# Attention decode on one core: the two heads of a tile on separate partition halves, one load each, and scores read at a smaller stride

## The chip, the cores and the metric

The kernel runs on one core of one Trainium2 chip. The metric is the device time of one execution in microseconds (us). Every experiment was timed beside the kernel before on the same chip.

Names used throughout: PE is TensorE (matmuls), PEld its weight loads, DVE is VectorE, ACT is ScalarE, POOL is GpSimd, SP is SyncE, which issues the loads. "Partition" means one of the 128 rows of the on-chip memory SBUF. "L330" is a line of the kernel file; matmuls are recorded by two helpers, so all ordinary matmuls share one line and are told apart by their tiles. The changed kernel is one line longer above the helpers, so L330, L334 and L660 of before are L331, L335 and L661 of after, and L332 and L662 in some experiments.

## The reference, cut to what matters

One decoding step for four sequences. Only the last 4096 of 16384 cached keys count. An FFN runs beside the attention, and a sigmoid gate mixes the two.

```python
def _A_ref(x, k_cache, v_cache, wq, wo):          # B=4, 32 query heads, 8 key heads, Dh=128
    W = min(4096, max(256, Sk // 4))              # 4096
    q = (x @ wq).reshape(B, 1, 32, 128)...        # transposed to B, heads, 1, 128
    k = repeat(k_cache[:, :, Sk - W:, :], 4, axis=1)
    v = repeat(v_cache[:, :, Sk - W:, :], 4, axis=1)
    scores = einsum("bhqd,bhkd->bhqk", q, k) * (Dh ** -0.5)
    o = einsum("bhqk,bhkd->bhqd", softmax(scores), v)
    return o.reshape(B, 1, 4096) @ wo
# b = ReGLU FFN of B_x (512 -> 1792 -> 512)
# result: g * a + (1 - g) * b, g = sigmoid(sum(x * gate_w))
```

Keys and values together are 67.1 MB, all weights 13.9 MB. Each byte is used for very little arithmetic, so the loads are the first thing to look at; the profile below shows that they set the pace.

## The kernel before

The work is cut into 16 tiles. A tile is one batch and two neighbouring key heads, with 2 MB of keys and 2 MB of values; two tiles make a set, and there are 8 sets. For each tile:

- one load of keys puts 64 keys of one head (16 KB) on each partition, with the two heads interleaved: partition 2r+h holds rows r of head h;
- PE transposes the tile as fp32 pairs of bf16, 32 products of 128x128, and DVE or ACT copies them back over the loaded keys;
- the score products of a set read those transposed keys, four column groups of PE at a time; DVE evicts them to `sc` with a running maximum; ACT computes the exponentials into `pe`, which is interleaved with zeros for the other head;
- PE transposes the probabilities and multiplies them with the value tile.

The parts that the change touches (cuts marked):

```python
def _pe_order():
    ...
        o += [("SC", s), ("OQ", i - 3), ("PV", i - 2), ("SW", s)]       # per set s; PV is the value tile
    ...

# in sync(): the loads
                load(("K", i), f"d_k{i % KSLOTS}", Ksb[:, i % KSLOTS, :],
                     A_k_cache[b, h:h + 2, SK - WIN:SK, :].rearrange("h (r c) d -> r h (c d)", r=64), waits=w)
    ...
                src = A_v_cache[b, h:h + 2, SK - WIN:SK, :].rearrange("h (r c) d -> r h (c d)", r=64)
                    load(("V", i), f"d_v{slot}", Vsb[:, slot, :], src, waits=w)
    ...

# in tensor(): the score products of set s
            for f in range(4):
                ...
                for e in range(2):
                    for j in range(4):
                        jp, pair = j // 2, j % 2              # jp: which head of the tile
                        ...
                        rhs = kt2((2 * s + pair) % KSLOTS)[:, 8 * f:8 * f + 8, jp:128:2, e]
                        mm(bk[32 * j:32 * j + 8, :], qblk[:, g, 8 * e:8 * e + 8], rhs, e == 0, e == 1,
                           ..., pos=(0, 32 * j))

# in scalar(): the exponentials, one for each head's 64 rows
        pev = pe[:, :].rearrange("p (k u) -> p k u", u=2)
                a.activation(pev[r, :, n], sc[r, :], ACTF.Exp, ...)
```

In `rhs`, `e` picks one bf16 of an fp32 pair and `jp:128:2` every second partition of the tile, so neighbouring elements lie 8 bytes apart.

## Time and profile before

| what | before | where it is read |
|---|---|---|
| time | 213.43 us at first, 213.54 us beside the changed kernel | timed runs |
| DMA engines busy | full from slice 2 to slice 36 of 40 | the page's slices |
| rate of the loads | about 425 GB/s | slices, window view |
| a 16 KB packet (one partition's row of a tile) | 0.61 us | DMA records of the trace |
| PE busy | 75% | the page's first part |
| PE waits for key loads | 17.3 us | view of waits |
| a score product | 629 ns (median) | view of one tile |

The first lines are the page of the kernel before: the span, the busy time of each engine, then a digit (busy tenths) or a rate for each of 40 equal slices of the span, and last the share of each engine in the chain of work that ended last.

```profile
span 209.9 us, 5524 instructions
...
PE 157.9 (75%) x2526; PEld 112.2 (53%) x2526; DVE 121.5 (58%) x279; ACT 69.8 (33%) x62; POOL 4.3 (2%) x19
...
DMA  5999999999999999999999999999999999998200
GB/s 206 419 456 400 419 433 419 434 437 417 428 395 408 440 422 425 434 425 428 418 434 418 428 428 425 436 409 426 425 431 422 428 431 425 425 418 353 81 0 4
...
PE 48%; DMA 25%; ACT 13%; DVE 9%; issue 2%; SPq 2%; ACTq 0%; DVEq 0%
```

The DMA engines never run dry before slice 37, and they move about 425 GB/s. The 35 full slices of 5.25 us at that rate are 78 of the 81 MB that have to be moved. The last line seems to say otherwise: PE holds 48% of the chain. The chain goes back through the wait of a load for its buffer, and so through PE, although many other loads were still under way.

The groups of instructions on the page of before: line, engine, operation, output<-input, shapes, count, then busy us, mean ns of one, and the engine's idle time just before them with what ended most of it.

```profile
L334 PE MATMUL bank<-identf,Ksb 128*128 128x128 f32 x512 | 72.5, 306 | 22.6 <-DMA Ksb<-in_A_k_cache_dram 17.3
...
L660 ACT ACTIVATE pe<-sc,negmax 64x2048 bf16<-64x2048 bf16 x16 | 41.6, 2600 | 49.1 <-DVE negmax L586 48.9
L330 PE MATMUL bank<-Ksb,qblk 128*8 128x512 bf16 x256 | 30.9, 623 | 4.7 <-DVE Ksb L533 4.7
```

These are the key transposes, the exponentials and the score products. The score products are 30.9 / 8 = 3.9 us of PE for each set.

The view of the key tile, for the score products of before (after the count: shortest, median and longest duration in ns):

```profile
L330 PE MATMUL bank<-Ksb,qblk x256: 608/629/662, 35.9 to 187.4; 128*8 128x512 bf16 x128
```

The waits of the queue's own engine in before (us in total, times, longest):

```profile
SPq L254 <- PE bank L330: 126.6, 10, 32.4
```

SP waits 126.6 us for PE to free buffers. That costs nothing, because enough loads are already queued, as the loads themselves show (issues on the page of before: count, KB each, median us from issue to landing):

```profile
Ksb<-in_A_k_cache_dram SPq DMA_DIRECT2D x16, 2048.0 KB, 25.0
Vsb<-in_A_v_cache_dram SPq DMA_DIRECT2D x15, 2048.0 KB, 31.7
Wbig<-in_A_wq_dram SPq DMA_DIRECT2D x1, 4096.0 KB, 16.5
```

2 MB at 425 GB/s are 4.9 us, and a key tile lands 25 us after its issue, so about five tiles are always in the queue.

### The profile page before, as it was taken

The numbers are of one execution on the slowest core, as the hardware profiler recorded it, in microseconds if no ns is written. First come the engines' busy times: TensorE is split into PE (matmuls) and PEld (weight loads), VectorE is DVE, ScalarE is ACT, GpSimd is POOL, SyncE is SP. The second block draws the span as 40 slices with busy tenths as digits, with TensorE's granted clock in tenths as the row PEclk, the third lists the DMA queues.
The fourth block names the chain that finished last, engine by engine and source line by source line (L and its number), as shares of the span: only waits on it lengthen the run. The fifth ranks groups of instructions, "written<-read, shape, count | busy, mean of one in ns | idle before, by whom it ended". The sixth has DMA issues, their size and how long they took to land.

```text
span 209.9 us, 5524 instructions
## 1 busy us (share of the span) xinstructions
PE 157.9 (75%) x2526; PEld 112.2 (53%) x2526; DVE 121.5 (58%) x279; ACT 69.8 (33%) x62; POOL 4.3 (2%) x19
## 2 busy tenths in 40 slices
PE   0373708889997129897896989698969899994784
PEld 0361506268376029276745947594759347842731
DVE  3180784789659005695678468736873647962312
ACT  2000411195036004172509143613362345508100
POOL 7000000000000000000000000000000000000000
PEclk9997976999999955997999799859975999998569
DMA  5999999999999999999999999999999999998200
GB/s 206 419 456 400 419 433 419 434 437 417 428 395 408 440 422 425 434 425 428 418 434 418 428 428 425 436 409 426 425 431 422 428 431 425 425 418 353 81 0 4
DMA packets 6839, 81.37 MB, mean 388 GB/s; under 512 B 792, under 2 KB 800, under 8 KB 2336
## 3 DMA queue, kind: packets, MB, share of 16 engines
q1 hardware_dynamic: 6816, 81.01, 91.5%
q8 instruction: 20, 0.33, 0.6%
q14 instruction: 3, 0.02, 0.0%
HBM read 81.01 MB, written 0.00 MB: 386 GB/s over the span
## 4 chain that ended last, share of the span: by engine, by line
PE 48%; DMA 25%; ACT 13%; DVE 9%; issue 2%; SPq 2%; ACTq 0%; DVEq 0%
PE bank L330 32%; DMA Ksb<-in_A_k_cache_dram 17%; PE bank L334 17%; ACT pe L660 13%; DMA Wbig<-in_A_wq_dram 8%; DVE Ksb L533 4%; DVE pe L565 2%; SPq L254 2%; DVE qblk L557 1%; DVE osb L600 1%; DVE negmax L586 0%; DVE osum L623 0%; DVE hmax L584 0%; DVE oq L607 0%; ACTq L95 0%
## 5 line engine op out<-in xcount | busy, mean ns | idle before, releaser
L334 PE MATMUL bank<-identf,Ksb 128*128 128x128 f32 x512 | 72.5, 306 | 22.6 <-DMA Ksb<-in_A_k_cache_dram 17.3
L533 DVE COPY Ksb<-bank 128x1024 bf16<-128x1024 bf16 x104 | 66.3, 685 | 33.6 <-PE bank L334 32.8
L334 PEld LDWEIGHTS bank<-identf,Ksb 128*128 128x128 f32 x512 | 66.4, 160 | 26.8 <-issue 10.2
L660 ACT ACTIVATE pe<-sc,negmax 64x2048 bf16<-64x2048 bf16 x16 | 41.6, 2600 | 49.1 <-DVE negmax L586 48.9
L637 ACT ACTIVATE Ksb<-bank 128x1024 bf16<-128x1024 bf16 x24 | 24.3, 1023 | 55.1 <-PE bank L334 55.1
L330 PE MATMUL bank<-Ksb,qblk 128*8 128x512 bf16 x256 | 30.9, 623 | 4.7 <-DVE Ksb L533 4.7
L575 DVE TENSOR_SCALAR_CACHE_REDUCE sc<-bank 128x512 bf16<-128x512 f32 x32 | 22.1, 692 | 14.0 <-PE bank L330 14.0
L330 PE MATMUL bank<-Vsb,pT 128*8 128x128 bf16 x1024 | 21.9, 245 | 2.3 <-issue 2.3
L330 PEld LDWEIGHTS bank<-Vsb,pT 128*8 128x8 bf16 x1024 | 17.9, 96 | 3.1 <-issue 2.7
L330 PEld LDWEIGHTS bank<-Ksb,qblk 128*8 128x8 bf16 x256 | 4.5, 88 | 25.0 <-DVE sc L575 13.4
L330 PE MATMUL bank<-sel,pe 128*128 128x32 bf16 x256 | 8.0, 181 | 11.6 <-ACT pe L660 11.3
L600 DVE TENSOR_SCALAR osb<-bank,recip 128x128 bf16<-128x128 f32 x16 | 5.6, 351 | 16.0 <-PE bank L330 15.5
L591 DVE CAST pT<-bank 128x512 bf16<-128x512 f32 x16 | 10.3, 685 | 6.6 <-PE bank L330 6.6
L330 PEld LDWEIGHTS bank<-sel,pe 128*128 128x128 bf16 x256 | 7.2, 99 | 12.8 <-DVE oq L607 8.2
L330 PE MATMUL bank<-Wbig,oq 128*4 128x512 bf16 x32 | 8.6, 425 | 0.7 <-DVE oq L607 0.7
L330 PEld LDWEIGHTS bank<-oneh,osb 128*32 128x32 bf16 x256 | 4.6, 115 | 7.0 <-issue 4.0
L330 PE MATMUL bank<-oneh,osb 128*32 128x2 bf16 x256 | 5.3, 176 | 1.3 <-DVE osb L600 1.3
L330 PE MATMUL bank<-rowsum,wsum 128*128 128x1 f32 x32 | 6.0, 292 | 0.0
L330 PE MATMUL bank<-Wbig,xT 128*4 128x512 bf16 x32 | 3.4, 603 | 3.4 <-DMA Wbig<-in_A_wq_dram 3.4
L330 PEld LDWEIGHTS bank<-rowsum,wsum 128*128 128x128 f32 x32 | 5.5, 242 | 0.1
L330 PEld LDWEIGHTS bank<-Wbig,oq 128*4 128x4 bf16 x32 | 2.7, 92 | 5.3 <-issue 1.8
L648 ACT ACTIVATE ge<-bank 4x1 f32<-4x1 f32 x2 | 0.2, 152 | 13.5 <-PE bank L330 13.5
(51 smaller groups left out, 47.5 us busy)
## 6 DMA issues: line engine op xcount, KB each, us to landing
Ksb<-in_A_k_cache_dram SPq DMA_DIRECT2D x16, 2048.0 KB, 25.0
Vsb<-in_A_v_cache_dram SPq DMA_DIRECT2D x15, 2048.0 KB, 31.7
Wbig<-in_A_wq_dram SPq DMA_DIRECT2D x1, 4096.0 KB, 16.5
Wbig<-in_A_wo_dram SPq DMA_DIRECT2D x1, 4096.0 KB, 31.5
Vsb<-in_A_v_cache_dram SPq DMA_DIRECT2D x4, 512.0 KB, 24.9
Vsb<-in_B_W_gate_dram SPq DMA_DIRECT2D x1, 1792.0 KB, 24.3
Vsb<-in_B_W_up_dram SPq DMA_DIRECT2D x1, 1792.0 KB, 33.1
Vsb<-in_B_W_down_dram SPq DMA_DIRECT2D x1, 1792.0 KB, 41.0
```

Source lines behind the costliest of these rows:

```text
L254: E.op(lambda: e.dma_start(dst, src), ev=ev, waits=waits, ctr=ctr)
L330: E.op(lambda: t.matmul(out_, lhsT, rhs, start=start, stop=stop, tile_position=pos, skip_group_check=True), ev=ev, waits=waits)
L334: E.op(lambda: t.transpose(out_, in_, idn), ev=ev, waits=waits)
L533: E.op(lambda: v.tensor_copy(kt_dst(i, f), bankb[tr(key)]), ev=("E",) + key, waits=[key])
L557: E.op(lambda r=r, u=u, b=b: v.tensor_copy(qv[r, b, n, :, :, :, u], src[r, :, :, b, :]), ev=("E",) + key if lastop else None, waits=[key, ...
L565: E.op(lambda n=n: v.memset(pev[64 * n:64 * n + 64, :, 1 - n], 0.0), ev=("PEZ",) if n else None, waits=[("QT", 1)])
L575: E.op(lambda: v.tensor_scalar(sc[:, 512 * f:512 * f + 512], banks[scb(key)], 1.0, None, op0=ALU.mult, op1=ALU.max, accum_out=mx4[:, f:f + ...
L591: E.op(lambda: v.tensor_copy(pT[:, s % 2, 512 * f:512 * f + 512], banks[tr(key)]), ev=("E",) + key, waits=[key] + ([("PV", 2 * s - 3)] if ...
L600: E.op(lambda: v.tensor_scalar(osb[:, i % 2, :], banks[OB][:, 0:128], recip[:, i % 4:i % 4 + 1], None, op0=ALU.mult), ev=("NORM", i), wait ...
L637: E.op(lambda: a.activation(kt_dst(i, f), bankb[tr(key)], ACTF.Copy), ev=("E",) + key, waits=[key])
L648: E.op(lambda u=u: a.activation(ge[:, u:u + 1], banks[ACC][0:4, 0:1], ACTF.Exp, scale=-1.0 if u == 0 else 1.0), ev=("GE",) if u else None, ...
L660: E.op(lambda r=r, n=n: a.activation(pev[r, :, n], sc[r, :], ACTF.Exp, bias=negmax[r, s % 2:s % 2 + 1], scale=SCALE, accum_out=rowsum[r, s ...
```

## The change

The intent is to make PE's reads of the keys denser. If head 0 lies on partitions 0 to 63 and head 1 on 64 to 127, the columns of one head are neighbours after the transpose, and the score products read at stride 2 (4 bytes) and not at stride 4 (8 bytes). Each tile then takes two loads of 1 MB, one for each head. The scores of a set are issued in two halves, with the output step and a value tile between them, so that PE has work while scores are evicted. The probabilities lie in blocks of 64 in place of every second element. The diff, cut to its core:

```diff
@@ _pe_order
-        o += [("SC", s), ("OQ", i - 3), ("PV", i - 2), ("SW", s)]
+        o += [("SC", s, 0), ("OQ", i - 3), ("PV", i - 2), ("SC", s, 1), ("SW", s)]
@@ sync, keys (values alike, also the pieces of the last tile)
-                load(("K", i), f"d_k{i % KSLOTS}", Ksb[:, i % KSLOTS, :],
-                     A_k_cache[b, h:h + 2, SK - WIN:SK, :].rearrange("h (r c) d -> r h (c d)", r=64), waits=w)
+                for j in range(2):
+                    load(("K", i, j), f"d_k{i % KSLOTS}", Ksb[64 * j:64 * j + 64, i % KSLOTS, :],
+                         A_k_cache[b, h + j, SK - WIN:SK, :].rearrange("(r c) d -> r (c d)", r=64), waits=w)
+                plan.ev[("K", i)] = plan.ev[("K", i, 1)]
@@ tensor, scores
-            for f in range(4):
+            for f in (2 * half, 2 * half + 1):
...
-                        rhs = kt2((2 * s + pair) % KSLOTS)[:, 8 * f:8 * f + 8, jp:128:2, e]
+                        rhs = kt2((2 * s + pair) % KSLOTS)[:, 8 * f:8 * f + 8, 64 * jp:64 * jp + 64, e]
@@ vector (memsets) and scalar (exponentials)
-        pev = pe[:, :].rearrange("p (k u) -> p k u", u=2)
+        pev = pe[:, :].rearrange("p (k u r) -> p k u r", u=2, r=64)
```

More of the change, by code (lines that the diff above doesn't have):

```diff
@@ L141, in _pe_order @@
 def _pe_order():
-    o = [("KT", 0), ("XT",), ("Z",), ("Q",), ("QT",), ("KT", 1), ("SC", 0), ("SW", 0)]
-    o += [("KT", 2), ("GU",), ("PT", 0), ("RS", 0), ("KT", 3), ("HT",), ("SC", 1), ("FFN",), ("SW", 1), ("PV", 0)]
+    o = [("KT", 0), ("XT",), ("Z",), ("Q",), ("QT",), ("KT", 1), ("SC", 0, 0), ("SC", 0, 1), ("SW", 0)]
+    o += [("KT", 2), ("GU",), ("PT", 0), ("RS", 0), ("KT", 3), ("HT",), ("SC", 1, 0), ("FFN",), ("SC", 1, 1), ("SW", 1), ("PV", 0)]
     for s in range(2, NSET):
@@ L222, in _program @@
         elif k == "SC":
-            for f in range(4):
+            for f in (2 * it[2], 2 * it[2] + 1):
                 scf[("SC", it[1], f)] = len(scf)
@@ L285, in sync @@
                     w += {WG_SLOT: [("GU", 1)], WU_SLOT: [("GU", 1)], WD_SLOT: [("FFN",)]}.get(slot, [])
-                src = A_v_cache[b, h:h + 2, SK - WIN:SK, :].rearrange("h (r c) d -> r h (c d)", r=64)
-                if i < NPAIR - 1:
-                    load(("V", i), f"d_v{slot}", Vsb[:, slot, :], src, waits=w)
-                else:
-                    n = TILE // VPIECES
-                    for p in range(VPIECES):
-                        load(("V", i, p), f"d_vl{p}", Vsb[:, slot, p * n:(p + 1) * n],
-                             src[:, :, p * n:(p + 1) * n], waits=w if p == 0 else [])
+                n = TILE // (VPIECES if i == NPAIR - 1 else 1)
+                for p in range(TILE // n):
+                    for j in range(2):
+                        src = A_v_cache[b, h + j, SK - WIN:SK, :].rearrange("(r c) d -> r (c d)", r=64)
+                        load(("V", i, p, j), f"d_v{slot}" if i < NPAIR - 1 else f"d_vl{p}",
+                             Vsb[64 * j:64 * j + 64, slot, p * n:(p + 1) * n], src[:, p * n:(p + 1) * n], waits=w)
+                    plan.ev[("V", i, p)] = plan.ev[("V", i, p, 1)]
         E.op(lambda: e.dma_start(out.rearrange("b o d -> (b o) d"), osum[0:4, :]), ev=("OUT",), waits=[("OSUM",)],
@@ L375, in QT, with SC @@
                        waits=tr_free(key) + [("E", "Q", n), ("QD", n)])
-        def SC(s):
+        def SC(s, half):
             b, qq = set_of(s)
-            for f in range(4):
+            for f in (2 * half, 2 * half + 1):
                 key = ("SC", s, f)
@@ L392, in SC @@
                            ev=key if lastmm else None, waits=w if (e, j) == (0, 0) else (), pos=(0, 32 * j))
-            plan.ev[("SCL", s)] = plan.ev[("SC", s, 3)]
+            plan.ev[("SCL", s)] = plan.ev[("SC", s, f)]
         def PT(s):
@@ L410, in PV @@
                     w = [("E", "PT", s, 0), ("INIT",)] + ([("NORM", i - 1)] if i else [])
-                    w += [("V", i)] if i < NPAIR - 1 else []
+                    w += [("V", i, 0)] if i < NPAIR - 1 else []
                 if ch == 32:
@@ L495, in _program @@
         elif k == "SC":
-            dve += [("ESC", it[1], f) for f in range(4)] + [("MAX", it[1])]
+            dve += [("ESC", it[1], f) for f in (2 * it[2], 2 * it[2] + 1)] + [("MAX", it[1])] * it[2]
         elif k == "SW":
@@ L562, in PEZ @@
         def PEZ():
-            pev = pe[:, :].rearrange("p (k u) -> p k u", u=2)
+            pev = pe[:, :].rearrange("p (k u r) -> p k u r", u=2, r=64)
             for n in range(2):
-                E.op(lambda n=n: v.memset(pev[64 * n:64 * n + 64, :, 1 - n], 0.0), ev=("PEZ",) if n else None,
+                E.op(lambda n=n: v.memset(pev[64 * n:64 * n + 64, :, 1 - n, :], 0.0), ev=("PEZ",) if n else None,
                      waits=[("QT", 1)])
@@ L632, in scalar @@
         E = _Eng(plan, a, "act")
-        pev = pe[:, :].rearrange("p (k u) -> p k u", u=2)
+        pev = pe[:, :].rearrange("p (k u r) -> p k u r", u=2, r=64)
         def EKT(i, f):
@@ L659, in EXP @@
                 w = [("NEGMAX", s), ("E", "SC", s, 3)] + ([("PT", s - 1, 1)] if s else []) + ([("RS", s - 2)] if s >= 2 else [("PEZ",)])
-                E.op(lambda r=r, n=n: a.activation(pev[r, :, n], sc[r, :], ACTF.Exp, bias=negmax[r, s % 2:s % 2 + 1],
+                E.op(lambda r=r, n=n: a.activation(pev[r, :, n, :], sc[r, :].rearrange("p (k r) -> p k r", r=64), ACTF.Exp, bias=negmax[r, s % 2:s % 2 + 1],
                                                    scale=SCALE, accum_out=rowsum[r, s % 2:s % 2 + 1]),
```

## The prediction

> **What bounds it now.** The loads. The page's slices show the DMA engines full and about 425 GB/s from the second slice to the 36th of 40; 81 MB at that rate are 190 us of a 209.9 us span. In the trace's DMA records a 16 KB packet (one partition's row of a tile) takes 0.61 us: 26.8 GB/s an engine, 429 for sixteen. The chain of waits names PE for 48%, but the DMA queue's own waits (127 us on PE) only delay issues: a key tile lands 25 us, a value tile 32 us after its issue, five or six tiles are always queued, and the engines never run dry. After the loads comes a tail: the last value pieces land near 195 to 198 us, the rest is PE and DVE work.
>
> **What the change removes.** Keys are read at 4 bytes instead of 8 between neighbours. Today a set's 32 score products take 3.85 us; four start together, each group 0.44 us after the last (timeline, 165 to 169 us), and every bank then waits for an eviction of 0.69 + 0.08 us. If stride 2 makes a group 0.22 us, evictions (4 x 0.77 = 3.1 us) become the limit, and the value tile between the halves fills that wait. Estimate: 1.5 to 2 us of PE a set, some 14 us in all, plus up to 3 us in the two early memsets (1.76 us each). Nearly all of it is off the critical path, since the loads set the pace; at most 3 to 5 us of the tail could be won. Exponentials and evictions keep their sizes.
>
> **What it adds.** Some 36 more DMA issues of about 0.5 us on the sync queue: hidden. But every key and value load now writes 64 partitions, first 0 to 63, then 64 to 127, in order in the same queue. [...]
>
> **Sum (estimate).** 13.9 MB of weights at 427 GB/s: 33 us. [...] With 2 us of start and 8 us of tail, 351 to 301 us. I expect about 312 us, 1.46 times the 213.43 us; range 245 to 355 us. Chances: slower by over 2% 0.84, within 2% 0.07, faster 0.09.
>
> **What would show it.** GB/s in the slices down to 220 to 280 while the DMA share stays high; 16 KB packets near 1.0 to 1.2 us; waits of PE's transposes on the key loads grown from 17 us to 80 or more; PE busy below 60%; the weight loads unchanged. Apart from that, score products (median 629 ns) near 300 to 400 ns and a set's score work below 3.3 us of PE.
>
> **What would make it wrong.** [...] the rate remains above 400 GB/s, and the shorter PE work gives 204 to 213 us.

The marked cuts take out what no trace of before shows: why a load on one half of the partitions would run slower, and at which rates. The sum came to 351 to 301 us, with the point at 312 us. One of its terms is cut, that of the 67.1 MB of keys and values; the terms that are left (33 us of weights, 2 us of start, 8 us of tail) make 43 us. No load of before writes only a half, and the prediction said itself that this step was unproved. It also counted on a relief: engines that have drifted to opposite halves were to run at full rate again. That was the author's guess; the trace of before shows only the drift, since the sixteen completions of one load spread over 0.5 us at first (8.0 to 8.5 us of the span) and over 4.0 us late (158.5 to 162.4 us). The conditions cut from the last paragraph are that half loads are not slower at all, or that the relief comes early and stays.

## More of the kernel before

The window view of before, 80 to 165 us of the span (its first line names the columns):

```profile
core 0: us, PE busy (x) PEld busy (x) DVE busy (x) ACT busy (x) POOL busy (x), PEclk, DMA share, GB/s
80.00:165.00 85.00, 73.08 (x1194) 56.39 (x1193) 57.48 (x128) 35.96 (x31) 0.00 (x0) 0.86 1.01 425
```

In this steady stretch PE is busy for 73 of 85 us and the DMA engines for all of it, at 425 GB/s.

## The result, and the profile after

The changed kernel took 350.2 us (median of 4 runs, 348.84 to 353.36) against 213.54 us (213.19 to 214.29) of the kernel before on the same chip. The ratio is 1.641, with a 95% interval of 1.629 to 1.653. Here and below a ratio is the mean time of one kernel's fast runs over that of the other's fast runs in the same rounds, so it is not quite the ratio of the medians that are quoted. The result is correct.

The page of after, the same parts:

```profile
span 346.1 us, 5566 instructions
...
PE 169.8 (49%) x2526; PEld 133.8 (39%) x2526; DVE 121.2 (35%) x279; ACT 61.2 (18%) x62; POOL 4.3 (1%) x19
...
DMA  8999999999999999999999999999999999999810
GB/s 182 319 347 252 265 312 206 308 218 214 204 347 285 214 216 216 237 233 231 229 220 223 225 223 228 218 235 220 228 254 259 267 254 261 279 271 247 210 47 0
...
DMA 63%; PE 20%; another core or an unknown queue 11%; SPq 2%; DVE 2%; issue 1%; DVEq 0%
```

The DMA row is as full as before, but the rate row is not: from slice 14 to 29 it averages 225 GB/s. The busy share says that the engines always have a packet in hand; it does not say that they move it at full speed. The higher early slices (319, 347, 312) are those with weight loads, which still span all 128 partitions: from 14 to 22 us of the span, with query weights under way, 393 GB/s are moved. The instruction counts of PE are the same, and PE's share of busy time fell from 75% to 49%.

The groups of after:

```profile
L335 PE MATMUL bank<-identf,Ksb 128*128 128x128 f32 x512 | 88.2, 353 | 115.6 <-DMA Ksb<-in_A_k_cache_dram 115.5
...
L661 ACT ACTIVATE pe<-sc,negmax 64x2048 bf16<-64x2048 bf16 x16 | 32.0, 1999 | 67.0 <-DVE negmax L587 66.8
...
L331 PE MATMUL bank<-Ksb,qblk 128*8 128x512 bf16 x256 | 22.3, 463 | 5.1 <-DVE Ksb L534 4.7
```

The transposes now wait 115.5 us for key loads; it was 17.3. The exponentials went from 2600 to 1999 ns and the score products from 623 to 463 ns on average. So what the change was made for came true. The value products wait too (waits of after, us in total, times, longest):

```profile
PE bank L335 <- DMA Ksb<-in_A_k_cache_dram: 115.5, 15, 21.7
...
PE bank L331 <- DMA Vsb<-in_A_v_cache_dram: 37.3, 14, 5.4
```

The view of the key tile of after, for the score products:

```profile
L331 PE MATMUL bank<-Ksb,qblk x256: 385/388/634, 39.4 to 317.7; 128*8 128x512 bf16 x128
```

The median is 388 ns; some are up to 634 ns. The granted clock averages 0.70 in the window from 100 to 300 us of after, where PE often waits, against 0.86 in the steady stretch of before, and the transposes have grown to 353 ns as well. That the clock explains both was not tested.

```profile
100.00:300.00 200.00, 98.54 (x1494) 81.08 (x1481) 70.36 (x157) 37.30 (x36) 0.00 (x0) 0.70 1.01 240
```

The loads on the page of after:

```profile
Ksb<-in_A_k_cache_dram SPq DMA_DIRECT2D x32, 1024.0 KB, 43.2
Vsb<-in_A_v_cache_dram SPq DMA_DIRECT2D x30, 1024.0 KB, 55.7
Wbig<-in_A_wq_dram SPq DMA_DIRECT2D x1, 4096.0 KB, 20.2
```

Half the size, and yet a key load lands 43 us after its issue, where the whole tile took 25. From the DMA records of the traces, the time of one packet in ns (5% / median / 95%), for this and for the experiments below:

```
16 KB packets   before              611 /  613 /  621
                after               822 / 1166 / 1288
                e2_opposite         966 / 1200 / 1274
                e4_values_only      611 / 1132 / 1288
                e8, both queues     909 / 1075 / 1283
                e9_stride_2         611 /  612 /  620
                e10, 114 to 138 us 1787 / 2104 / 2412
```

A packet of the same size takes about twice as long after the change. The extra time agrees with that: 67.1 MB at 426 GB/s are 157.5 us; with the 136.7 us that were added they are 294 us, which would be 228 GB/s (an estimate that puts the whole difference on the keys and values).

### The profile page after: what moved, and what is told of

Same layout as the page of the kernel before. It is cut to its first block, busy times and chain, and to the rows that moved or that the text cites. A ratio compares the mean times of both kernels' runs of the same rounds, so it can differ in the third digit from the quotient of the medians.

```text
span 346.1 us, 5566 instructions
## 1 busy us (share of the span) xinstructions
PE 169.8 (49%) x2526; PEld 133.8 (39%) x2526; DVE 121.2 (35%) x279; ACT 61.2 (18%) x62; POOL 4.3 (1%) x19
## 4 chain that ended last, share of the span: by engine, by line
DMA 63%; PE 20%; another core or an unknown queue 11%; SPq 2%; DVE 2%; issue 1%; DVEq 0%
DMA Ksb<-in_A_k_cache_dram 49%; DMA Vsb<-in_A_v_cache_dram 14%; PE bank L331 10%; PE bank L335 9%; SPq L254 2%; DVE Ksb L534 1%; DVE sc L576 0%; DVE osum L624 0%; DVE osb L601 0%; DVE oq L608 0%; DVE rowmax L580 0%; DVEq L67 0%
## 5 line engine op out<-in xcount | busy, mean ns | idle before, releaser
L335 PE MATMUL bank<-identf,Ksb 128*128 128x128 f32 x512 | 88.2, 353 | 115.6 <-DMA Ksb<-in_A_k_cache_dram 115.5
L335 PEld LDWEIGHTS bank<-identf,Ksb 128*128 128x128 f32 x512 | 84.2, 190 | 118.5 <-issue 62.4
L534 DVE COPY Ksb<-bank 128x1024 bf16<-128x1024 bf16 x104 | 68.7, 688 | 142.7 <-PE bank L335 142.1
L661 ACT ACTIVATE pe<-sc,negmax 64x2048 bf16<-64x2048 bf16 x16 | 32.0, 1999 | 67.0 <-DVE negmax L587 66.8
L331 PE MATMUL bank<-Vsb,pT 128*8 128x128 bf16 x1024 | 24.1, 260 | 37.5 <-DMA Vsb<-in_A_v_cache_dram 37.3
L331 PEld LDWEIGHTS bank<-Vsb,pT 128*8 128x8 bf16 x1024 | 19.7, 102 | 39.5 <-DMA Vsb<-in_A_v_cache_dram 34.0
L331 PE MATMUL bank<-Ksb,qblk 128*8 128x512 bf16 x256 | 22.3, 463 | 5.1 <-DVE Ksb L534 4.7
L331 PE MATMUL bank<-Wbig,oq 128*4 128x512 bf16 x32 | 10.9, 510 | 0.6 <-DVE oq L608 0.6
L331 PEld LDWEIGHTS bank<-Ksb,qblk 128*8 128x8 bf16 x256 | 6.1, 96 | 13.2 <-DVE Ksb L534 6.1
L331 PE MATMUL bank<-rowmax,perm 128*128 128x1 bf16 x8 | 1.4, 180 | 8.7 <-DVE rowmax L580 8.7
## 6 DMA issues: line engine op xcount, KB each, us to landing
Wbig<-in_A_wq_dram SPq DMA_DIRECT2D x1, 4096.0 KB, 20.2
```

The source lines that it names most:

```text
L331: E.op(lambda: t.matmul(out_, lhsT, rhs, start=start, stop=stop, tile_position=pos, skip_group_check=True), ev=ev, waits=waits)
L335: E.op(lambda: t.transpose(out_, in_, idn), ev=ev, waits=waits)
L534: E.op(lambda: v.tensor_copy(kt_dst(i, f), bankb[tr(key)]), ev=("E",) + key, waits=[key])
L661: E.op(lambda r=r, n=n: a.activation(pev[r, :, n, :], sc[r, :].rearrange("p (k r) -> p k r", r=64), ACTF.Exp, bias=negmax[r, s % 2:s % 2 + 1],
```

## The experiments

The theory at this point: the cost lies in where the rows of a load stand. Loads that write only partitions 0 to 63, or only 64 to 127, move at 225 GB/s in the middle slices of after; loads over all 128 move at 425 in before. The rivals: (A) it is the number of loads, their size, or the order in which the cache is read; (B) it is something else in the change, such as the order on PE or the layout of the probabilities. The theory also had a second part, the relief, which was a guess: when the engines drift apart, some write the first half while others write the second, and the two groups should not disturb each other. All the experiments below but e1 gave correct results.

### e1: the changed kernel with loads over the full width

The same 32 loads of 1 MB for the keys, from the same addresses, but each over 128 partitions, with half rows of 8 KB. The keys then stand in the wrong place, and the result is wrong (relative error 0.729).

```diff
-    load(("K", i, j), ..., Ksb[64 * j:64 * j + 64, i % KSLOTS, :],
-         A_k_cache[b, h + j, SK - WIN:SK, :].rearrange("(r c) d -> r (c d)", r=64), waits=w)
+    load(("K", i, j), ..., Ksb[:, i % KSLOTS, 4096 * j:4096 * j + 4096],
+         A_k_cache[b, h + j, SK - WIN:SK, :].rearrange("(r c) d -> r (c d)", r=128), waits=w)
# values alike
```

> The changed kernel with one thing undone: each of its two loads a tile writes all 128 partitions (half of the columns) instead of 64 partitions; same number of loads, 1 MB each, from the same contiguous source of one head. The result is wrong on purpose (keys and values lie in other places). Theory [...]: 205 to 212 us, 420 GB/s or more, 8 KB packets near 0.31 us. Rival A (two smaller loads a tile, or reading one head's contiguous region at a time, is what costs): 330 us or more, as in the changed kernel. Whatever it gives is also the worth of the change without its loads.

It took 210.95 us (209.46 to 212.52), a ratio of 0.9884 (0.9811 to 0.9956) to before. From its page, the rates, the score products and the key loads:

```profile
GB/s 217 488 402 396 439 413 426 421 417 424 416 414 407 420 421 421 418 419 421 419 422 421 416 421 424 416 418 421 416 421 421 421 418 419 418 424 398 253 9 1
...
L332 PE MATMUL bank<-Ksb,qblk 128*8 128x512 bf16 x256 | 18.4, 389 | 5.0 <-DVE Ksb L535 4.7
...
Ksb<-in_A_k_cache_dram SPq DMA_DIRECT2D x32, 1024.0 KB, 22.9
```

The whole loss is gone. Rivals A and B are out: the number of loads, their size and their source are the same, and so is the rest of the change. The rest of the change is worth 1.2%. PE's score work fell from 30.9 to 18.4 us, 12.5 us in all, and the time fell by some 2.5 us, because PE did not set the pace.

### e2 and e3: two groups of engines on opposite halves

If the relief is real, it can be forced. The second head is loaded first, and the first load of the kernel is cut so that 8 engines get more of it than the other 8; from then on one group should stay ahead and write one half while the other writes the other half. In e2 the extra is 4 rows for each of the 8 engines, half of an engine's 8 rows of a tile (128 rows over the sixteen engines whose completions the trace shows); in e3 it is 8 rows, a whole tile.

```diff
-    for j in range(2):
+    for j in (1, 0):
+        # tile 0, j == 1, e2: rows 0:32 in one load, rows 32:64 in four loads of 8 rows, 4 apart
+        #   Ksb[96 + t:125 + t:4, ...] <- src[32 + t:61 + t:4]            for t in 0..3
+        # e3: all 64 rows in eight loads of 8 rows, 4 apart
+        #   Ksb[64 + g:93 + g:4, ...] <- src[g:g + 29:4]                  for g in 0..3, 32..35
```

> The changed kernel, still 64 partitions a load. Second head first, and 32 of the first load's 64 rows go on 8 engines alone, so that these 8 run half a tile behind the other 8 from the start. Theory [...] the rate is near 400 GB/s at first and falls with drift: 215 to 260 us. Rival B (a load of 64 partitions runs at half rate for a reason that has nothing to do with which engines are in the same half[...]): 335 to 355 us.

> As e2, but all 64 rows of the first load go on the 8 engines, so that these run a whole tile (both halves) behind. Theory: a whole period is no offset[...]: 325 to 350 us. If e2 was fast for having a few odd loads at the start, or for engines merely being apart, this is as fast as e2.

This missed altogether. e2 took 358.97 us (357.22 to 360.87), a ratio of 1.680 (1.672 to 1.689): slower than the changed kernel itself. e3 took 357.36 us in its fast run; its profiled run of 363.96 us was slow, so it adds nothing but that it is no better. The completions in e2's trace show two groups of eight engines some 2.8 us apart in the first 50 us; a half takes about 4.9 us there, so the groups are in opposite halves for a little over half of that time. Later the sixteen completions of a load spread evenly over some 5 us. Two windows of e2: in the short one the ahead group has ended a key load on partitions 64 to 127 (at 27.3 to 27.6 us) and writes 0 to 63, while the other group is still on 64 to 127 (until 30.1 us); the long one is the steady part.

```profile
27.60:30.10 2.50, 2.50 (x20) 0.99 (x12) 1.17 (x4) 0.83 (x2) 0.00 (x0) 0.50 1.00 210
100.00:300.00 200.00, 94.24 (x1463) 77.24 (x1462) 66.15 (x151) 36.25 (x35) 0.00 (x0) 0.70 1.01 228
```

Even there the rate is 210 GB/s, and every 16 KB packet takes 1.2 us or more. So standing on opposite halves did not bring the pace back. Why not was not shown: which rows an engine takes in a load of 64 rows is not recorded in the profile.

### e4: only the values in halves

The kernel before with the change's value loads and the layout of the probabilities, and with its own key loads over all 128 partitions.

```diff
-    load(("V", i), f"d_v{slot}", Vsb[:, slot, :], src, waits=w)
+    for j in range(2):
+        src = A_v_cache[b, h + j, SK - WIN:SK, :].rearrange("(r c) d -> r (c d)", r=64)
+        load(("V", i, p, j), ..., Vsb[64 * j:64 * j + 64, slot, p * n:(p + 1) * n], src[:, p * n:(p + 1) * n], waits=w)
# keys and scores as before; pe in blocks of 64
```

> The kernel before with only the values in two loads of 64 partitions; key loads, score products at stride 4 and their order as before. Theory: [...] 275 to 290 us, 16 KB packets of two sorts, near 0.61 and 1.25 us. Rival C (the score side of the change matters for the loss): 213 to 220 us.

It took 319.77 us (318.46 to 321.09), ratio 1.497 (1.487 to 1.506), more than the 275 to 290 us expected. (An estimate: 33.5 MB of values at the 225 GB/s of after, and not at the 425 of before, add 70 us to 213.83 us, which makes 284 us.) Two windows of e4: before the value loads dominate, and in the steady part.

```profile
10.00:50.00 40.00, 30.97 (x344) 21.10 (x342) 28.05 (x66) 12.06 (x15) 0.00 (x0) 0.91 1.00 400
150.00:250.00 100.00, 56.32 (x766) 47.24 (x766) 38.38 (x80) 17.57 (x17) 0.00 (x0) 0.68 1.01 227
```

With equal parts of full-width and half-width loads in the queue, the rate is 227 GB/s, that of the halves alone (225 in after). From 200 to 220 us of the span the 16 KB packets of both sorts take between 1046 and 1273 ns (5% to 95%), so the key packets, which go to all partitions, are slowed as well. A likely reading, not shown, is that the engines do not run in step: while some still write a half, others have begun the next load, and these are held to the same pace. This is the first sign of a third theory: loads on a half set the pace of all that is under way, full-width loads too.

### e5: heads by column, so that the loads stay whole

A design that gets the denser reads with no half loads. Each partition holds 32 keys of the first head and 32 of the second, in one load over 128 partitions with rows of 8 KB. The scores of a head read a block of columns at 4 bytes between neighbours, one exponential covers 128 rows, and the transposes of the probabilities halve, since there are no zeros.

```diff
+    load(("K", i), ..., Ksb[:, i % KSLOTS, :].rearrange("p (j x) -> p j x", j=2),
+         A_k_cache[b, h:h + 2, SK - WIN:SK, :].rearrange("j (p c) d -> p j (c d)", p=128), waits=w)
-    rhs = kt2(...)[:, 8 * f:8 * f + 8, 64 * jp:64 * jp + 64, e]
+    rhs = kt2(...)[:, 16 * jp + 4 * f:16 * jp + 4 * f + 4, :, e]
# EXP: pe[:, 0:2048] <- sc[:, :] in one instruction; PT one fill of 16; PV with 4 columns a head
```

> Another layout with the same aim: both heads on all 128 partitions, each in its own half of the columns (32 keys a partition), one load a tile. Score products read at stride 2, scores in two halves as in the change; no zero blocks, so one exponential of 128 rows a set instead of two of 64, half of the probability transposes. Expected if loads at full width are all that the change lacked: loads as before (425 GB/s to 195 us), tail some 4 to 7 us shorter: 204 to 209 us, result right. If the layout costs load rate (8 KB rows): 213 us or more.

It took 210.37 us (210.0 to 211.08), ratio 0.9894 (0.9841 to 0.9947): faster than before and correct, but by less than was expected. The rates of e5:

```profile
GB/s 209 458 421 382 437 416 427 438 411 418 415 412 408 418 426 421 420 418 418 421 423 412 424 418 427 415 412 421 423 423 420 416 420 421 421 423 397 278 12 1
```

They are near 420 GB/s where before had 425. In the trace an 8 KB packet takes 312 ns, which is 1.02 of half a 16 KB packet (613 ns). The last value piece lands near 200 us, and in before near 197.5. So part of what PE gained was given back to the loads, and the kernel is still bound by them.

### e6: the order on PE alone

The kernel before with the scores split around the value tile, and nothing else.

```diff
-        o += [("SC", s), ("OQ", i - 3), ("PV", i - 2), ("SW", s)]
+        o += [("SC", s, 0), ("OQ", i - 3), ("PV", i - 2), ("SC", s, 1), ("SW", s)]
```

> The kernel before with only the order of the change: scores in two halves around a value tile, stride 4 and loads as before. The loads bound it, so 212 to 214 us; if PE were the bound as the chain of waits says, some 8 times 1 to 1.5 us less: 202 to 206 us.

It took 214.25 us (212.38 to 214.79), ratio 1.0064 (1.0009 to 1.012). The order brings no time; if anything it costs 0.6%. The chain of before gives PE 48%, and a better order of PE's work returns nothing from it: while loads are queued several tiles deep, PE's place in the chain is not a measure of what PE costs.

### e7: one load for both heads, heads outermost

The changed kernel with its two key loads of a tile made one, with the same places in SBUF.

```diff
-    for j in range(2):
-        load(("K", i, j), ..., Ksb[64 * j:64 * j + 64, ...], ...)
+    load(("K", i), ..., Ksb[:, i % KSLOTS, :],
+         A_k_cache[b, h:h + 2, SK - WIN:SK, :].rearrange("h (r c) d -> h r (c d)", r=64), waits=w)
```

> The changed kernel with one load a key tile in the same layout (heads outermost in the source; value loads in halves as in the change). [...] two engines carry 33.5 MB of keys at 26.8 GB/s each, 626 us, with their share of the rest 740 to 815 us. If it is sprayed over 16 engines instead, 128 partitions at once: 270 to 290 us.

It took 876.18 us (one look, state not known), more than the 740 to 815 us expected of two engines at their full pace. In the trace two engines report the end of each key load, where sixteen do in before, and 54 GB/s move while they are alone. More telling are the moments when other loads share the time with them. Four windows of e7: the first keys beside the query weights, keys alone, query and FFN weights with no keys, and keys beside FFN weights.

```profile
6.00:22.00 16.00, 0.00 (x0) 0.00 (x0) 0.00 (x0) 0.00 (x0) 0.00 (x0) 1.00 0.98 230
25.00:49.00 24.00, 0.00 (x0) 0.00 (x0) 0.00 (x0) 0.00 (x0) 0.00 (x0) 1.00 0.13 54
52.00:57.00 5.00, 5.00 (x28) 5.00 (x27) 3.87 (x6) 0.00 (x0) 0.00 (x0) 1.00 0.97 346
69.00:75.00 6.00, 0.00 (x0) 0.00 (x0) 1.82 (x2) 0.00 (x0) 0.00 (x0) 0.58 1.02 238
```

From 6 to 22 us two engines carry keys and the other 14 carry weights over the full width, and all together move 230 GB/s. A 32 KB packet of weights takes about 2.3 us there; in before it takes 1.21. From 52 to 57 us the same two engines carry query weights instead, and a 14 KB packet of the FFN weights has its full pace (median 535 ns, as in before); beside keys, from 69 to 75 us, it takes 1006 ns. So while two engines write keys, the 14 others run at half their pace. Why was not shown.

### e8: the second head's loads from another queue

The changed kernel with the loads of the first head issued by SP and those of the second by GpSimd, each with its own semaphores, meant to have the two halves written side by side.

```diff
-    for j in range(2):        # both heads, one queue, on SP
+    for j in js:              # SP: js = (0,)   GpSimd: js = (1,)
```

> The changed kernel with the second head's loads issued from GpSimd, so that both halves are queued at once on two queues. If the engines alternate between the queues packet by packet[...]: 240 to 300 us. If the queues do not help[...]: 330 to 360 us.

It took 342.2 us (342.04 to 342.35), ratio 1.609 (1.595 to 1.623). That is 8 us less than the changed kernel, and far from a cure.

### e9: two loads a tile of 64 partitions each, but every second one

The kernel before, its layout untouched, with its one load of a tile made two: the first head on partitions 0, 2, 4 and so on, the second on 1, 3, 5.

```diff
-    load(("K", i), ..., Ksb[:, i % KSLOTS, :], <both heads, 128 rows>, waits=w)
+    for j in range(2):
+        load(("K", i, j), ..., Ksb[j:127 + j:2, i % KSLOTS, :], <one head, 64 rows>, waits=w)
# values alike
```

> The kernel before, layout and score side untouched, with two loads a tile, one a head: 64 partitions each, but every second one (0, 2, 4 ... and 1, 3, 5 ...), so each load reaches both halves [...]; 16 KB rows, 1 MB, sources as in the changed kernel. [...] 213 to 225 us. [...] 300 to 350 us.

The first range is for the case that the reach over both halves is what counts, the second for the case that a load of 64 rows is slow wherever they stand.

It took 212.83 us (212.56 to 213.09), ratio 1.0016 (0.9914 to 1.0118), where the fast runs of before on that chip had a mean of 212.5 us (several others counted as slow and are left out). The steady window of e9:

```profile
80.00:165.00 85.00, 73.83 (x1189) 57.54 (x1187) 56.09 (x126) 34.70 (x30) 0.00 (x0) 0.83 1.01 426
```

These are the change's own loads in number, size, source and rows (64 of 16 KB each), at 426 GB/s. All that differs in the loads is which partitions the 64 rows stand on. With e1 this settles the cause of the loss: it is on which partitions a load's rows stand. That the reach over both halves is what counts, and not the step of 2 in itself, is the author's reading; a load of 64 neighbours across the middle (32 to 95) was not tried.

### e10: loads of eight neighbouring rows, made on purpose

The kernel before, with the 4 MB of output weights loaded in 16 loads of 8 rows. The first eight loads take rows 4 apart, the second eight take 8 neighbouring rows. The loads of keys and values stay over all 128 partitions.

```diff
+    for t in range(8):
+        g = 32 * (t // 4) + t % 4 if it[1] == 0 else 64 + 8 * t
+        r = slice(g, g + 29, 4) if it[1] == 0 else slice(g, g + 8)
+        load(("WO", it[1], t), "d_wo", dst[r], src[r], waits=[("Q",)])
```

> The kernel before; only the load of the output weights (4 MB) is cut into 16 loads of 8 partitions, each carried by 8 engines. The first 8 loads (near 65 us) write partitions 4 apart in 0 to 63[...]; the second 8 (some 40 us later) write 8 neighbouring partitions each in 64 to 127[...]. The other 8 engines meanwhile go on with key and value tiles at full width. [...] their 16 KB packets stay at 0.61 us in the first stretch[...]. [...] in the second stretch all of them are slowed, to 0.9 us or more. Time 222 to 260 us, the packets are what counts.

Two outcomes were named for the second stretch: nearly all of the tile packets on the other engines keep their 0.61 us, or all of them are slowed.

It took 250.13 us (one look, state not known). Windows of e10 with the first eight loads under way (their 4 KB packets run from 59.6 to 72 us of the span), and with the second eight:

```profile
60.00:70.00 10.00, 8.66 (x211) 7.90 (x213) 7.65 (x16) 5.30 (x4) 0.00 (x0) 0.88 0.98 382
114.00:138.00 24.00, 3.65 (x100) 3.38 (x100) 2.92 (x7) 1.50 (x2) 0.00 (x0) 0.53 1.00 121
```

Eight rows 4 apart leave the rate at 382 GB/s, and the 16 KB packets of the tile loads keep their 611 ns (median). Eight neighbouring rows bring it down to 121 GB/s for all sixteen engines, though these loads are only a part of what is under way: 16 KB packets of the tile loads take 1.8 to 2.4 us (5% to 95%). The records do not name the engine, but each eight-row load is completed by eight engines and no 16 KB packet took under 1.65 us, so those of the other eight engines were slow too. So engines are slowed that carry none of the eight-row loads, which the prediction had left out. That the neighbouring rows in SBUF do it is the likely reading and not the only one: the second eight loads also read neighbouring rows of the source, 4 KB apart and not 16 KB, and write the upper half, and no run separates these.

### e11 and e12: can more be had?

e11 is e5 with the second part of the output product after the last value tile.

```diff
-    o += [("WO", 1), ("PV", i + 3), ("OQ", i + 3), ("WO", 2)]
+    o += [("PV", i + 3), ("WO", 1), ("OQ", i + 3), ("WO", 2)]
```

> e5 with the second part of the output product (8 products, 2.4 us) after the last value tile instead of ahead of it: the last value tile ends earlier and the part fills the wait for its normalisation. 1 to 2 us less than e5: 208.5 to 209.5 us.

It took 210.04 us (209.5 to 210.6), ratio 0.9889 (0.983 to 0.9948), 0.3 us below e5 and not told apart from it; 1 to 2 us had been expected.

e12 keeps the loads of before and makes the heads neighbours in the transposing product, by a permuted identity matrix in place of the plain one (column 64h+r takes partition 2r+h). The scores then read 4 bytes apart, with nothing else paid. The scores are split as in the change; the layout of the probabilities is that of before.

```diff
+    aff(identp[:, :], ones[:, :], [[-1, 2], [-2, 64]], 0, eq, 0.0, ("IDP",), [("ONES",)])
-    tp(bk[...], kf[...], identf[:, :], ...)
+    tp(bk[...], kf[...], identp[:, :], ...)
-    rhs = kt2(...)[:, 8 * f:8 * f + 8, jp:128:2, e]
+    rhs = kt2(...)[:, 8 * f:8 * f + 8, 64 * jp:64 * jp + 64, e]
```

> The kernel before with its loads untouched (128 partitions, 16 KB rows, heads interleaved), and the score side of the change: the product that transposes a key tile takes a permuted identity, so that the two heads come out in separate halves of the 128 columns and the scores read at stride 2; scores in two halves around a value tile. If the transposing product honours the permutation the result is right, and the time is that of e1 (1.2% under the kernel before) or a little less, since 16 KB rows load some 1.6% faster than 8 KB rows: 208 to 211.5 us. If stride 2 brings nothing that e6 did not: 213 to 215 us. A wrong result would mean that the transposing product ignores the permutation.

It took 211.35 us (210.23 to 212.6) against 212.73 us, ratio 0.9916 (0.9825 to 1.0007). That points the right way, and the interval just includes no gain. Two groups of e12:

```profile
L662 ACT ACTIVATE pe<-sc,negmax 64x2048 bf16<-64x2048 bf16 x16 | 41.6, 2600 | 42.3 <-DVE negmax L588 42.1
...
L332 PE MATMUL bank<-Ksb,qblk 128*8 128x512 bf16 x256 | 18.5, 389 | 5.0 <-DVE Ksb L535 4.7
```

The score products are as fast as in e1 (389 ns), while the exponentials, which write every second element here, stay at 2600 ns. e4, with keys and scores as in before and `pe` in blocks of 64, is the reverse:

```profile
L659 ACT ACTIVATE pe<-sc,negmax 64x2048 bf16<-64x2048 bf16 x16 | 32.0, 1999 | 56.6 <-DVE negmax L585 56.4
...
L329 PE MATMUL bank<-Ksb,qblk 128*8 128x512 bf16 x256 | 31.0, 624 | 4.7 <-DVE Ksb L532 4.7
```

So the two gains in the change have two separate causes: the stride of the keys, and the layout of the probabilities.

The versions that beat both kernels are e5 and e11, by about 1.1%, with intervals that exclude no gain.

## Why the prediction was right or wrong

The prediction said slower, 312 us with a range of 245 to 355. Measured were 350.2 us: the direction is right, the value is inside the range and 38 us above the point.

What held, step by step:

- "The loads" bound the kernel before, and the PE share of the chain is not a cost. e6 shows the second and e1 the first: 12.5 us less of score work on PE gave some 2.5 us.
- "Every key and value load now writes 64 partitions", and this costs the rate. e1 and e9 show that it is where the loads write and no other part of the change: the same number of loads, of the same size, run at about 420 GB/s over all 128 partitions (e1) and at 426 on every second one (e9). The prediction marked this as unproved in the trace of before, and it was.
- The upper end of the sum, 351 us, is close to the 350.2 us measured. That agreement is partly luck: this end stood for one rate throughout and for weights at 427 GB/s, while the measured rate is 225 GB/s in the middle slices and 254 to 279 in slices 30 to 36, and the weights did not stay at full speed.
- Of the signs, GB/s at 220 to 280 with a full DMA row came true for most slices. So did 16 KB packets of 1.0 to 1.2 us (median 1.17), transposes waiting for keys over 80 us (115.5), PE below 60% (49%), score products of 300 to 400 ns (median 388), and score work below 3.3 us a set (22.3 / 8 = 2.8).
- "At most 3 to 5 us of the tail could be won" by the shorter PE work: e1 shows 1.2%, about 2.5 us.

What failed is one step, and it is the one that set the point: the relief, which was a guess. The point of 312 us stands for 67.1 MB in 312 - 43 = 269 us, a mean of 249 GB/s. The runs put about 228 in its place (the estimate above). The engines do drift apart, but the drift does not pay: in e2, with the groups set some 2.8 us apart at the start, the time was 359 us and not less, and while the groups were in opposite halves a packet still took 1.2 us or more. e4, e7 and e10 show what the prediction lacked: loads at full width are slowed too, by others that are under way. Full-width loads beside half loads fall to 227 GB/s (e4), 14 engines run at half their pace beside two that write keys (1006 ns for a packet of 535, e7), and with loads of eight neighbouring rows under way everything falls to 121 GB/s (e10). What inside the chip does this was not shown.

Two smaller errors:

- "Exponentials and evictions keep their sizes" is wrong for the exponentials: 2600 to 1999 ns, since their output is now contiguous in blocks of 64. e4 and e12 show that this is the layout of `pe` and not something else. The two memsets fell from 1765 to 912 ns with the same layout, in which the profile shows them as 64x1024 uint32 and no longer as 64x2048 bf16. What this is worth in time was not measured alone; the loads set the pace.
- "The weight loads unchanged" held in part. A 32 KB packet still has a median of 1218 ns (before: 1213), but at 95% it takes 1646 ns, and the query weights land 20.2 us after their issue and not 16.5. Half loads share the queue with them, and in e4 such company slowed full-width packets to 1046 to 1273 ns where before has 613.

What stays open: which rows one engine takes in a load of 64 rows, which the profile does not record; why engines that carry other loads are slowed as well (e4, e7, e10); why the rate of the changed kernel rises to 254 to 279 GB/s late in the span (e8 shows 256 to 266 there); and the 11% of its chain that the profile puts down to "another core or an unknown queue".

## What to carry to other kernels

When a layout is changed for the sake of one engine's reads, first ask which partitions each load writes: here loads on 64 neighbouring partitions brought the rate from 425 GB/s to 225, and to 227 where half of the data still came at full width (e4), while 64 partitions at step 2 ran at the full 426 GB/s (e9). Read the DMA row together with the GB/s row, since full engines at half the rate look the same in the first. And where loads are queued several tiles deep, look for the layout on the engine's side instead, such as a permuted transpose (e12) or heads by column (e5), and expect little in return (0.8 to 1.1% here).
